# Attention's first q and k loaded raw, with heads on partitions, ahead of a weight fold in a one-core attention and feed-forward kernel

## The chip, the cores and the metric

The kernel runs on one core of a Trainium2 chip. The metric is the device time of one execution in microseconds (us); the median of several executions is quoted. The profile is one such execution; its span (first to last instruction) is about 1.7 us shorter than the time of the same execution (202.8 beside 204.56).

Engines: PE is the matrix engine (TensorE), PEld its weight loads, DVE the vector engine, ACT the scalar engine, POOL the engine that issues the casting loads (the software queue), SP the engine that issues the raw loads, the transposing DMAs and the stores (the hardware queue).

## The reference

```python
# q, k, v: [4 batches, 8 heads, 768 positions, 64], float32
scores = q @ k.T / sqrt(64)                    # keep 4 sink positions and a window of 128
a = softmax(where(keep, scores, -1e9))
x = (a @ v) as [3072 tokens, 512]
out = (((x @ w1) * (x @ w2)) @ w3) @ w_out     # w1, w2 [512,1024], w3 [1024,1024], w_out [1024,512]
```

Nothing nonlinear stands between w3 and w_out, so the kernel first folds them into `w3o = w3 @ w_out` (an extra product at the start, a shorter one for every token afterwards). That fold needs w3 (4 MB) and w_out (2 MB) early. Attention needs only 1.5 MB for its first tile of 256 positions of batch 0 ("tile 0"). These loads share the first 25 us (DMA share 1.13 to 2.13 from 5 to 25 us in the windows of the kernel before; the share is explained there).

## The kernel before

The order of all PE, ACT, DVE and SP instructions is fixed when the program is built: a small model in the kernel guesses when each load lands and how long each step takes, and emits the work in the order of that model. If the matrix engine would idle in the first 40 us by the model, it emits filler matmuls (`keep_busy`, tile `pz`), meant to keep the engine's clock up.

```python
# POOL casts while loading: float32 in memory, bf16 in SBUF
def rows(src, b, kb):                       # 128 positions; runs of 64 floats = 256 B
    return src[b, :, kb * P:(kb + 1) * P, :].rearrange("h p d -> p h d")

order = [('w3', 0, 2, 1, 2), ('w3', 2, 4, 1, 2), ('wo', 1), ('qkv', 0, 0, 2), ('w3', 6, 8, 0, 2),
         ('qkv', 0, 2, 4), ('w3', 5, 6, 0, 2), ('w3', 4, 5, 0, 2), ('w1', 0), ('w2', 0), ('w1', 1),
         ('w2', 1), ('qkv', 0, 4, 6), ('qkv', 1, 0, 6), ('qkv', 2, 0, 6), ('qkv', 3, 0, 6)]
# ... four raw loads on SP, cast afterwards by DVE and ACT:
def load_raw(dst, src, i0, tile_):
    nc.sync.dma_start(out=tile_, in_=src[i0 * P:(i0 + 2) * P, 0:512].rearrange("(ko ki) n -> ki ko n", ki=P))
    return dst[:, i0:i0 + 2, 0:512], tile_
casts = [load_raw(w3_sb, moe_w3, 0, raw(0, 0)), load_raw(wo_sb, moe_w_out, 0, raw(1, 0)),
         load_raw(wo_sb, moe_w_out, 2, raw(1, 1)), load_raw(w3_sb, moe_w3, 2, raw(0, 1))]
# ... cut ...
def transposes(src, dst, t):                # q or k of 256 positions to [head dim, position]
    tp = ps_mm.tile([P, NP, 2, P], BF16, tag="mm", name="tp")
    for r in range(NP):
        for i in range(2):
            nc.tensor.transpose(tp[:, r, i, :], src[:, 2 * t + i, r * P:(r + 1) * P], ident[:])
    yield
    nc.vector.tensor_copy(dst[:, :, t * 256:(t + 1) * 256], tp[:].rearrange("p r i m -> p r (i m)"))
    yield
# ... cut: scores, values, gates, fold, project; the model; the emission ...
```

The softmax here doesn't subtract the row's maximum and nothing guards it: scores larger than these inputs give would overflow.

## Time and profile before

| | before |
|---|---|
| time, median (lowest to highest) | 204.73 us (204.12 to 204.88, 3 runs) |
| span of the profiled execution | 202.2 us |
| last matmul ends | 198.6 us |
| idle + fillers of PE up to 26 us | 4.9 + 9.9 us |
| idle of PE from 26 us to the last matmul | 0.9 us |
| first scores | 24.2 us |

The split into idle, fillers and wanted work is my sum over the trace: a matmul counts from its start to the start of the next one, at most for its own duration; what lies between is idle. (The prediction's own reading of the same timeline, 15.4 and 1.1 us, was done by hand.)

These are lines of the table of windows of the kernel before: the window in us, its length, then busy us and number of instructions of PE, PEld, DVE, ACT, POOL, the granted PE clock as a share of full speed, the DMA share (the times of all packets added up, over 16 engines; packets overlap, and it reaches 2.13 here), and GB/s written. The clock of the first window is not to be trusted: no clock is on record before 5.3 us, and the fillers follow each other every 0.43 us until then and every 0.22 afterwards.

```profile
0.00:5.00 5.00, 3.67 (x9) 1.34 (x10) 2.19 (x5) 1.28 (x1) 3.23 (x9) 1.00 0.56 151
5.00:10.00 5.00, 4.92 (x28) 2.36 (x27) 3.15 (x8) 1.12 (x2) 2.98 (x6) 1.00 1.13 295
10.00:15.00 5.00, 2.36 (x19) 1.32 (x20) 0.77 (x3) 2.01 (x2) 5.00 (x7) 1.00 1.51 223
15.00:20.00 5.00, 5.00 (x33) 2.63 (x33) 1.72 (x8) 0.30 (x1) 4.86 (x8) 1.00 2.13 171
...
25.00:30.00 5.00, 4.95 (x57) 3.30 (x57) 3.79 (x11) 3.15 (x5) 4.53 (x7) 1.00 1.54 194
```

From 25 us on PE is busy all the time; only the start has slack. "Busy" includes fillers, which the timeline of PE separates. It gives start, duration, operation, output and inputs, count, and in brackets the idle time before the group and what ended it:

```profile
1.33 5.98 PE L376 MATMUL pz<-ksbd_113 128*128 128x512 bf16 x18 [1.33 <-DVE ksbd_113 L146]
7.15 0.39 PE L333 MATMUL tp_259<-ident,w_sb 128*128 128x128 bf16 x4
...
13.80 0.40 PE L333 MATMUL tp_291<-ident,w_sb 128*128 128x128 bf16 x4 [1.33 <-ACT w_sb L163]
...
22.17 0.61 PE L191 MATMUL tp<-ident,kN_86 128*128 128x128 bf16 x8
22.62 0.61 PE L191 MATMUL tp<-ident,qN_82 128*128 128x128 bf16 x8
...
24.16 0.51 PE L245 MATMUL sc<-qT_94,kT_98 64*128 64x256 bf16 x8 [0.28 <-DVE qT_94 L194]
```

The fold (`tp_…`, `ph`) comes first and waits piece by piece for weights; q and k of tile 0 are transposed only at 22.2 us. In the first 26 us about 15 us are fillers or idle. That is what a change of the load order can win.

The part of the page that lists DMA issues (size each, median us from issue to landing):

```profile
ab_106<-in_moe_w_dram SPq DMA_DIRECT2D x2, 512.0 KB, 7.5
ab_107<-in_moe_w_out_dram SPq DMA_DIRECT2D x2, 512.0 KB, 6.9
```

Of the four raw 512 KB loads the first landed at 5.4 us and the last at 12.7.

### The profile page before, as it was taken

The numbers are of one execution on the slowest core, as the hardware profiler recorded it, in microseconds if no ns is written. First come the engines' busy times: TensorE is split into PE (matmuls) and PEld (weight loads), VectorE is DVE, ScalarE is ACT, GpSimd is POOL, SyncE is SP. The second block draws the span as 40 slices with busy tenths as digits, with TensorE's granted clock in tenths as the row PEclk, the third lists the DMA queues.
The fourth block names the chain that finished last, engine by engine and source line by source line (L and its number), as shares of the span: only waits on it lengthen the run. The fifth ranks groups of instructions, "written<-read, shape, count | busy, mean of one in ns | idle before, by whom it ended". The sixth has DMA issues, their size and how long they took to land.

```text
span 202.2 us, 4514 instructions
## 1 busy us (share of the span) xinstructions
PE 192.7 (95%) x1800; PEld 120.7 (60%) x1813; DVE 109.9 (54%) x263; ACT 107.0 (53%) x180; POOL 74.1 (37%) x97
## 2 busy tenths in 40 slices
PE   7949899999999999999999999999999999999992
PEld 2425466698886885576666655566665466554440
DVE  4613288665897773467878654877775044440000
ACT  2231556755765866777666664666663433333331
POOL 6699494488999963622770000000000000000000
PEclk9999999999999999999999999999999999999999
DMA  5999999999999999999999994502021610002333
GB/s 154 294 219 173 165 197 206 192 156 154 154 150 151 161 144 126 214 175 204 155 132 157 118 161 129 159 5 52 3 52 67 192 55 2 0 3 104 150 145 120
DMA packets 102773, 27.04 MB, mean 134 GB/s; under 512 B 95072, under 2 KB 98144, under 8 KB 102752
## 3 DMA queue, kind: packets, MB, share of 16 engines
q0 software_dynamic: 78624, 13.64, 91.5%
q1 hardware_dynamic: 24128, 13.11, 29.9%
q8 instruction: 14, 0.23, 0.5%
q14 instruction: 7, 0.06, 0.1%
HBM read 29.36 MB, written 6.29 MB: 176 GB/s over the span
## 4 chain that ended last, share of the span: by engine, by line
PE 87%; DMA 7%; ACT 2%; issue 1%; DVE 1%; SPq 1%; ACTq 0%
PE pg L316 42%; PE po L362 19%; PE av L276 7%; PE sc L245 6%; DMA ab_106<-in_moe_w_dram 5%; PE pw L351 3%; PE tp L191 2%; PE ph L351 2%; DMA xT_104<-xn 2%; PE xt L292 1%; PE pz L376 1%; PE sp L226 1%; ACT w3o L355 1%; SPq L140 1%; ACT w_sb L163 1%
## 5 line engine op out<-in xcount | busy, mean ns | idle before, releaser
L316 PEld LDWEIGHTS <-w_sb 128*128 128x128 bf16 x576 | 53.0, 98 | 25.5 <-issue 1.6
L323 ACT COPY a_sb<-pg 128x384 f32<-128x384 f32 (+1 forms) x72 | 32.0, 445 | 35.2 <-PE pg L316 15.0
L250 ACT ACTIVATE ex<-sc 128x1024 bf16<-128x1024 f32 (+1 forms) x48 | 44.8, 955 | 7.6 <-PE sc L245 7.0
L254 DVE TENSOR_TENSOR am<-ex,maskt 128x1024 bf16<-128x1024 bf16 (+1 forms) x48 | 30.3, 641 | 4.4 <-ACT ex L250 4.2
L366 ACT COPY o_sb<-po 128x512 f32<-128x512 f32 x24 | 14.1, 586 | 26.9 <-PE po L362 26.7
L316 PE MATMUL pg<-xT_102,w_sb 128*128 128x256 bf16 x192 | 24.3, 273 | 0.0
L316 PE MATMUL pg<-xT_103,w_sb 128*128 128x384 bf16 x128 | 23.7, 326 | 0.0
L316 PE MATMUL pg<-xT_104,w_sb 128*128 128x384 bf16 x128 | 22.6, 326 | 0.4 <-DMA xT_104<-xn 0.4
L283 DVE TENSOR_TENSOR xn<-av,rec 128x256 bf16<-128x256 f32 x48 | 20.4, 424 | 4.1 <-DMA xT_104<-xn 2.5
L316 PE MATMUL pg<-xT_105,w_sb 128*128 128x384 bf16 x128 | 21.0, 326 | 0.0
L276 PEld LDWEIGHTS <-am 128*128 128x128 bf16 x352 | 17.0, 97 | 3.3 <-issue 0.3
L320 DVE TENSOR_TENSOR ab_109<-a_sb,pg 128x384 bf16<-128x384 f32 x16 | 8.8, 553 | 17.1 <-PE pg L316 17.1
L280 DVE RECIPROCAL rec<-av 128x4 f32<-128x4 f32 x48 | 8.6, 180 | 16.5 <-PE av L276 16.2
L320 DVE TENSOR_TENSOR ab_106<-a_sb,pg 128x256 bf16<-128x256 f32 x24 | 10.0, 418 | 5.7 <-PE pg L316 4.2
L376 PE MATMUL pz<-ksbd_113 128*128 128x512 bf16 x36 | 10.5, 444 | 1.4 <-DVE ksbd_113 L146 1.3
L362 PE MATMUL po<-w3o,ab_106 128*128 128x512 bf16 x45 | 11.2, 379 | 0.2
L320 DVE TENSOR_TENSOR ab_108<-a_sb,pg 128x384 bf16<-128x384 f32 x16 | 8.9, 554 | 4.4 <-PE pg L316 1.6
L362 PE MATMUL po<-w3o,ab_107 128*128 128x512 bf16 x46 | 10.9, 379 | 0.1
L351 PEld LDWEIGHTS <-w3t 128*128 128x128 bf16 x64 | 6.0, 97 | 8.3 <-issue 2.0
L362 PE MATMUL po<-w3o,ab_108 128*128 128x512 bf16 x46 | 10.6, 379 | 0.1
L362 PE MATMUL po<-w3o,ab_109 128*128 128x512 bf16 x47 | 10.5, 379 | 0.1
L320 DVE TENSOR_TENSOR ab_107<-a_sb,pg 128x384 bf16<-128x384 f32 x16 | 8.8, 552 | 2.7 <-ACT ex L250 1.5
(143 smaller groups left out, 254.4 us busy)
## 6 DMA issues: line engine op xcount, KB each, us to landing
out_dram<-o_sb SPq DMA_DIRECT2D x24, 256.0 KB, 2.1
w_sb<-in_moe_w_dram POOLq DMA_DIRECT2D x5, 512.0 KB, 10.1
ab_106<-in_moe_w_dram SPq DMA_DIRECT2D x2, 512.0 KB, 7.5
w_sb<-in_moe_w_dram POOLq DMA_DIRECT2D x4, 256.0 KB, 8.3
ab_107<-in_moe_w_out_dram SPq DMA_DIRECT2D x2, 512.0 KB, 6.9
kN_86<-in_k_dram POOLq DMA_DIRECT2D x6, 128.0 KB, 8.8
qN_82<-in_q_dram POOLq DMA_DIRECT2D x6, 128.0 KB, 8.6
vN_90<-in_v_dram POOLq DMA_DIRECT2D x6, 128.0 KB, 8.5
```

Source lines behind the costliest of these rows:

```text
L245: nc.tensor.matmul(sc[:, e, c:c + n], kT[b][hp, r, kb * P:(kb + 1) * P], qT[b][hp, r, qb * P:qb * P + n], start=True, stop=True)
L250: nc.scalar.activation(ex[:, :, c0:], sc[:, :, c0:], ACTF.Exp, scale=scale)
L254: nc.vector.tensor_mul(am[:, :, c0:], ex[:, :, c0:], mk)
L276: nc.tensor.matmul(o, lhs, rhs, start=(n == 0), stop=(n == len(todo) - 1), skip_group_check=True)
L283: nc.vector.tensor_mul(xns[b, t][:, :, r, :, :], av[:, :, :, 0:D], rec[:].to_broadcast([P, 2, 2, D]))
L316: nc.tensor.matmul(pg[:], w_sb[:, kk, dt * P:(dt + 1) * P], xT[b][:, kk, tk], start=(kk == 0), stop=(kk == NP - 1))
L320: nc.vector.tensor_mul(ab[b][:, dt, tk], gate_a.pop((b, c, dt))[:], pg[:])
L323: nc.scalar.copy(a_sb[:], pg[:])
L351: nc.tensor.matmul(po, w3T[i][:, j, :], wo_sb[:, j, :], start=(j == 0), stop=(j == KFF - 1))
L362: nc.tensor.matmul(po[:], ab[b][:, kk, m * P:(m + 1) * P], w3o[:, kk, :], start=(kk == 0), stop=(kk == KFF - 1))
L366: nc.scalar.copy(o_sb[:], po[:])
L376: nc.tensor.matmul(pz[:], idle[:, 0:P], idle[:, 0:512], start=True, stop=True)
```

## The change

The intent: start with attention instead of the fold. k and q of tile 0 are loaded raw (float32, no cast) as the first two loads, in runs of 16 rows (4 KB). Partition p then holds head p // 16 and the run p % 16 of that head. PE transposes these tiles in float32, and the copies out of PSUM ("untangle") put the columns in order and cast them. Both DVE and ACT copy from each PSUM tile. w3 comes by whole rows of blocks, w_out in two column halves so that half a fold can start, w1 and w2 in quarters, and the other q, k of batch 0 in 512 B runs of two positions ("paired").

```diff
+    def run(src, b, t):
+        return src[b, :, 256 * t:256 * t + 256, :].rearrange("h (g j) d -> h g (j d)", j=16)
+
+    def pairs(src, b, t):
+        return src[b, :, 256 * t:256 * t + 256, :].rearrange("h (p j) d -> p h (j d)", j=2)
 ...
-    order = [('w3', 0, 2, 1, 2), ('w3', 2, 4, 1, 2), ('wo', 1), ('qkv', 0, 0, 2), ...
+    raw_order = [("k",), ("q",), ("w3", 0)]
+    order = [("w3", 2), ("wo", 0, 256), ("w3", 6), ("w3", 5), ("v", 0, 0), ("w3", 3), ("wo", 256, 512), ("w2", 0,
+             256), ("w1", 0, 256), ("w3", 1), ("k", 0, 1), ("q", 0, 1), ("w1", 256, 512), ("w3", 7), ...
 ...
+            nc.sync.dma_start(out=raw(n), in_=run({"k": k, "q": q}[what], 0, 0))
 ...
+    def transposes_raw(src, part, box):          # two parts of four, for k and for q
+        tp = ps_mm.tile([P, 4, P], FP32, tag="mm", name="tpr")
+        for n in range(4):
+            c = (4 * part + n) * P
+            nc.tensor.transpose(tp[:, n, :], src[:, c:c + P], ident32[:])
+        box.append(tp)
+        yield
+
+    def untangle(dst, part, e, box):             # e = 0 on DVE, e = 1 on ACT, same tile
+        tv = box[0][:].rearrange("p n (r e g) -> p e r g n", r=NP, e=2)
+        dv = dst[:, :, 0:256].rearrange("p r (g n j) -> p r g n j", g=16, n=8)
+        for j in range(2):
+            (nc.scalar.copy if e else nc.vector.tensor_copy)(
+                dv[64 * e:64 * e + 64, :, :, 4 * part:4 * part + 4, j], tv[64 * j:64 * j + 64, e])
+        yield
 ...  (cut: paired transposes, fold in column halves with the copy on DVE or ACT, sink scores
       merged into the scores task, new landing model and priorities)
```

## The prediction

> **What bounds the kernel now.** The table of windows has TensorE busy about 98% from 26 to 198.6 us: that part is its own work. The start is not: the timeline of TensorE up to 26 us holds about 10.6 us of wanted matmuls (weight transposes 8 x 0.22, fold matmuls 4 x 1.73, sink values 0.23, q/k transposes 0.9, scores 0.44). The other 15.4 us are idle or fillers (group pz; 18 of them fill 1.3 to 7.1 us). Later idle time is about 1.1 us, then 3.5 us of tail. Span 202.2 = 15.4 + about 182 useful + 1.1 + 3.5. Only the 15.4 us can be attacked.
>
> The start waits for data: the raw weight loads land at 5.4, 7.0, 9.9 and 12.7 us, the first q and k only at about 22. The windows show about 155 GB/s written while q, k, v come in 256-byte destination rows, 205 for casting weight rows; a casting load reads twice what it writes, so 0.31 and 0.41 MB/us are read, about 0.33 in the mixed raw stage.
>
> **What changes.** Raw k and q of tile 0 come first, so attention can start before the fold; w3 comes by rows, w_out in two column halves, so that half a fold (0.86 us) can run on half of w_out; w1, w2 in quarters; other batch-0 q, k in 512-byte source runs; the weight casts (3 x 1.04 us on ACT) go.
>
> Added TensorE work: 24 fp32 transposes, estimated at twice a bf16 one (0.055 us pipelined), +1.3 us; paired transposes, 16 instead of 8 per tile and tensor, four times, +0 to +1.8 us. Sink scores and values cost the same. About +2 us, all on the critical engine.
>
> **Start, worked out from those rates.** k lands at 5.2 to 6.5 us, q at 7 to 9: [...] these loads may get 8 engines of 16. No run yet shows it. First w_out half about 13 us, v of tile 0 about 17.5, second half about 22. By then about 11 us of work can be done; after that the backlog of second halves (4 to 5 us), the first gates and later w3 rows should keep TensorE full. So 11 to 12 us not useful instead of 15.4: 3.5 to 4.5 saved, about 2 given back; a little more from fewer small gaps and retuned priorities. Later stages unchanged within 1 us, whatever ACT and DVE save, because TensorE is full.
>
> **Prediction: 201.6 us, 198.6 to 204.4 (8 in 10). Faster by over 2%: 0.33; within 2%: 0.64; slower by over 2%: 0.03.**
>
> **What would show it.** First wanted matmul near 6 us instead of 7.1; first scores at 9 to 11 us instead of 24; first av at 17 to 19; fillers plus idle up to 26 us about 12; TensorE full from about 22 us; an fp32 transpose near 0.11 us pipelined; later stages as before.
>
> **What would make it wrong.** Faster: larger runs give 0.4 MB/us from the start, so w_out and v come 2 to 3 us earlier; paired transposes overlap fully. Slower: [...] raw loads crowd the casting queue; the strided untangling copies hold PSUM; landing guesses miss and TensorE stalls in its static order.

3.5 to 4.5 us saved less about 2 given back is 1.5 to 2.5 us, and the "little more" makes up the rest of the way from 204.7 to 201.6. The landings and the factor of two for a float32 transpose were my estimates; the factor was borne out by the runs (0.109 us each in g16_part, 0.056 for a bf16 one in the kernel before).

## The result

| | before | after |
|---|---|---|
| time, median (lowest to highest) | 204.43 us (203.76 to 204.88, 4 runs) | 210.11 us (209.61 to 211.29, 4 runs) |
| ratio of the fast runs | | 1.0294, interval 1.0256 to 1.0332 |
| span of the profiled execution | 202.2 us | 208.7 us |
| first scores | 24.2 us | one matmul at 19.2 us, the others from 20.2 |
| PE idle + fillers up to 26 us | 4.9 + 9.9 us | 8.7 + 8.5 us |

A ratio is the mean time of one kernel's fast runs over that of the other's of the same rounds, so it is not quite the ratio of the medians. The change made the kernel 2.9% slower. The prediction (201.6, range 198.6 to 204.4) was wrong.

The same windows after:

```profile
0.00:5.00 5.00, 3.67 (x10) 1.38 (x11) 2.92 (x11) 1.28 (x1) 3.81 (x11) 1.00 0.43 94
5.00:10.00 5.00, 2.78 (x17) 1.61 (x16) 0.08 (x1) 0.41 (x1) 4.95 (x10) 1.00 1.20 209
10.00:15.00 5.00, 1.29 (x6) 0.39 (x4) 2.01 (x8) 1.30 (x4) 0.76 (x1) 0.97 1.58 189
15.00:20.00 5.00, 3.98 (x25) 3.63 (x26) 2.51 (x6) 1.57 (x4) 0.81 (x2) 0.69 1.43 206
...
25.00:30.00 5.00, 4.54 (x65) 3.69 (x63) 3.48 (x11) 2.55 (x4) 1.82 (x3) 1.00 1.44 198
```

PE is less busy than before from 5 to 20 us, and the granted clock falls (0.69 in 15 to 20 us). The timeline of PE says what it waited for:

```profile
1.33 5.38 PE L428 MATMUL pz<-ksbd 128*128 128x512 bf16 x17 [1.33 <-DVE ksbd L170]
8.93 1.06 PE L246 MATMUL tpr<-ident,ab 128*128 128x128 f32 x8 [2.22 <-DMA ab<-in_k_dram]
9.83 1.46 PE L428 MATMUL pz<-ksbd 128*128 128x512 bf16 x6
15.38 1.94 PE L246 MATMUL tpr<-ident,ab 128*128 128x128 f32 x8 [4.09 <-DMA ab<-in_q_dram]
17.11 1.98 PE L393 MATMUL tp<-ident,ab 128*128 128x128 bf16 x16
19.23 0.27 PE L300 MATMUL sc<-qT,kT 64*128 64x256 bf16 x1
20.18 0.49 PE L300 MATMUL sc<-qT,kT 64*128 64x256 bf16 x7 [0.68 <-ACT qT L255]
...
22.65 1.92 PE L404 MATMUL pw<-wo_sb,w3t 128*128 128x256 bf16 x16
```

k landed at 8.9 us and q at 15.3, where 5.2 to 6.5 and 7 to 9 were predicted. The same eight transposes took 1.06 us for k and 1.94 for q, because the clock had halved meanwhile (0.5 on record from 14.7 to 18.1 us). The fold products (`pw`) start only at 22.7 us. That is not w_out's doing alone: its first half landed at 18.4 us, and from then on PE works, in its fixed order, through w3's transposes, the scores with their wait for q's copies, and 1.7 us of fillers. The chain of waits of the changed kernel has the same three parts in order (start, duration, what):

```profile
1.66 13.58 DMA ab<-in_q_dram
15.24 0.14 issue
15.38 1.10 PE tpr L246 x4
16.48 0.02 issue
16.50 0.42 ACT qT L255
...
17.40 0.42 DVE qT L255
...
19.27 0.42 ACT qT L255
```

So there are three suspects: the load of q (13.6 us from issue to landing), the copies, in which ACT and DVE take turns (16.50 to 20.14 us for q), and the clock. Wanted PE work also grew. Sums over all matmuls of the profiled executions, as defined above:

| us | before | after | g16 | g16_part |
|---|---|---|---|---|
| idle, before the last matmul | 4.6 + first 1.3 | 8.1 + 1.3 | 3.6 + 1.3 | 1.6 + 1.3 |
| fillers | 9.9 | 8.5 | 10.9 | 8.8 |
| wanted work | 182.9 | 187.2 | 187.4 | 185.9 |
| of it: transposes of q and k on PE | 5.6 | 7.6 | 6.7 | 6.7 |
| of it: transposes of w3 | 3.9 | 4.7 | 5.0 | 4.4 |
| last matmul ends | 198.6 | 205.1 | 203.3 | 197.6 |

(12 of the 256 fold and project matmuls of the kernel before are missing from its trace, which hides some tenths of a us of its work. The runs g16 and g16_part are explained below; the profiled execution of g16 is the slowest of its five, 208.67 us, and that of g16_part the fastest of its four, so these two columns lie further apart than the medians.)

### The profile page after: what moved, and what is told of

It is laid out like the page before. It is cut to its first block, busy times and chain, and to the rows that moved or that the text cites. A ratio compares the mean times of both kernels' runs of the same rounds, so it can differ in the third digit from the quotient of the medians.

```text
span 208.7 us, 4640 instructions
## 1 busy us (share of the span) xinstructions
PE 195.7 (94%) x1862; PEld 127.3 (61%) x1862; DVE 115.5 (55%) x273; ACT 106.7 (51%) x183; POOL 71.2 (34%) x96
## 4 chain that ended last, share of the span: by engine, by line
PE 85%; DMA 7%; DVE 5%; ACT 1%; issue 0%; SPq 0%; ACTq 0%; DVEq 0%
PE pg L374 40%; PE po L414 20%; PE pw L404 7%; PE av L334 7%; DMA ab<-in_q_dram 7%; PE sc L300 6%; PE xt L350 1%; PE tp L220 1%; DVE qT L255 1%; ACT qT L255 1%; PE tp L234 1%; PE pz L428 1%; PE tp L393 1%; PE sp L294 1%; DVE kT L237 1%; PE tpr L246 1%
## 5 line engine op out<-in xcount | busy, mean ns | idle before, releaser
L374 PE MATMUL pg<-xT,w_sb 128*128 128x384 bf16 (+1 forms) x576 | 90.1, 308 | 0.1
L378 DVE TENSOR_TENSOR ab<-a_sb,pg 128x384 bf16<-128x384 f32 (+1 forms) x72 | 36.4, 508 | 28.2 <-PE pg L374 26.5
L414 PE MATMUL po<-w3o,ab 128*128 128x512 bf16 x192 | 43.7, 379 | 0.3 <-DVE qT L223 0.3
L414 PEld LDWEIGHTS <-ab 128*128 128x128 bf16 x192 | 18.2, 98 | 20.4 <-issue 0.4
L341 DVE TENSOR_TENSOR xn<-av,rec 128x256 bf16<-128x256 f32 x48 | 20.4, 425 | 1.7
L114 POOL DMA_DIRECT2D qN<-in_q_dram x18 | 16.3, 905 | 9.5 <-DMA vN<-in_v_dram 4.4
L334 PE MATMUL av<-vN,am 128*128 128x65 bf16 x352 | 19.1, 193 | 0.1
L114 POOL DMA_DIRECT2D vN<-in_v_dram x18 | 16.1, 918 | 7.4 <-DMA kN<-in_k_dram 7.2
L338 DVE RECIPROCAL rec<-av 128x4 f32<-128x4 f32 x48 | 8.6, 178 | 18.1 <-PE av L334 18.0
L114 POOL DMA_DIRECT2D kN<-in_k_dram x18 | 16.3, 910 | 4.0 <-DMA qN<-in_q_dram 2.9
L404 PE MATMUL pw<-wo_sb,w3t 128*128 128x256 bf16 x128 | 15.4, 273 | 0.2 <-DVE w3t L213 0.2
L300 PE MATMUL sc<-qT,kT 64*128 64x128 bf16 (+1 forms) x256 | 14.3, 238 | 0.9 <-ACT qT L255 0.7
L404 PEld LDWEIGHTS <-w3t 128*128 128x128 bf16 x128 | 11.9, 98 | 2.4 <-DVE w3t L213 0.5
## 6 DMA issues: line engine op xcount, KB each, us to landing
w_sb<-in_moe_w_dram POOLq DMA_DIRECT2D x8, 256.0 KB, 10.4
```

The source lines that it names most:

```text
L114: nc.gpsimd.dma_start(out=dst, in_=rows(src, b, kb))
L300: nc.tensor.matmul(sc[:, e, c:c + n], kT[b][hp, r, kb * P:(kb + 1) * P], qT[b][hp, r, qb * P:qb * P + n], start=True, stop=True)
L334: nc.tensor.matmul(o, lhs, rhs, start=(n == 0), stop=(n == len(todo) - 1), skip_group_check=True)
L341: nc.vector.tensor_mul(xns[b, t][:, :, r, :, :], av[:, :, :, 0:D], rec[:].to_broadcast([P, 2, 2, D]))
L374: nc.tensor.matmul(pg[:], w_sb[:, kk, dt * P:(dt + 1) * P], xT[b][:, kk, tk], start=(kk == 0), stop=(kk == NP - 1))
L378: nc.vector.tensor_mul(ab[b][:, dt, tk], gate_a.pop((b, c, dt))[:], pg[:])
```

## Experiments

Theory, a guess of mine before the runs: how many DMA engines a load gets goes with its slowest dimension. The two loads have 8 heads there, so k and q would run on 8 of the 16 engines, and everything queued behind them on those 8 would be late too. Rivals: the casting queue crowds the raw loads; the landing guesses make PE stall in a bad order; the raw form (float32 transposes, copies) or attention first is itself the loss; the layout (a head's runs on neighbouring partitions) is slow.

### g16: the 16 runs of a head slowest

```diff
-  rearrange("h (g j) d -> h g (j d)", j=16)     # source [8, 16, 1024]
+  rearrange("h (g j) d -> g h (j d)", j=16)     # source [16, 8, 1024]
-  tv = box[0][:].rearrange("p n (r e g) -> p e r g n", r=NP, e=2)
+  tv = box[0][:].rearrange("p n (g r e) -> p e r g n", r=NP, e=2)
```

> The changed kernel with one thing altered: raw k and q of tile 0 lie on the partitions with the 16 runs of a head as the slow dimension and the 8 heads as the fast one (slowest dimension of the source 16 instead of 8), untangled accordingly. Same bytes, same runs, same instructions. Theory (the two loads run on 8 of the 16 DMA engines, and everything queued behind them on those 8 is late too): k lands at 5.2 to 6 us instead of 8.9, q at 7 to 8 instead of 15.3, the first w_out half at about 13 to 14 instead of 18.6, the clock does not fall, and the time is 200 to 203.5 us. Rival (the casting queue crowds the raw loads, or the extra fp32 work costs the time): q still lands after 12 us and the time is 208 us or more.

Measured: 207.43 us (206.99 to 208.67), ratio 1.0118 (1.0080 to 1.0156). Lines of its issues (size, us to landing), k issued at 0.80 and q at 1.55 us:

```profile
ab<-in_k_dram SPq DMA_DIRECT2D x1, 512.0 KB, 4.8
ab<-in_q_dram SPq DMA_DIRECT2D x1, 512.0 KB, 7.3
```

k lands at 5.6 us and q at 8.9: the landing part of the theory holds, and crowding alone is refuted, since the casting queue was the same. The order of the 1862 matmuls of PE is the same in both traces, so no change of order hides in the difference. But the time fell by 2.7 us only, and the clock fell in spite of the expectation (0.5 from 14 to 20.8 us in the profiled execution, the slowest; by their mean clock of 0.988 to 0.992 the other four lost less). Something else held PE. Its trace shows the copies in turns, and PE waiting for them:

```profile
12.63 0.86 ACT L255 CAST qT<-tpr 64x256 bf16<-64x256 f32 x2
...
13.53 1.77 DVE L255 CAST qT<-tpr 64x256 bf16<-64x256 f32 x4 [1.87 <-ACT qT L255]
14.54 1.08 PE L393 MATMUL tp<-ident,ab 128*128 128x128 f32 x4 [1.22 <-DVE qT L255]
15.39 0.86 ACT L255 CAST qT<-tpr 64x256 bf16<-64x256 f32 x2 [1.89 <-DVE qT L255]
```

Fillers that the program placed for the full clock then ran at the half one and stood in the way: seven took 3.17 us here, and 1.69 in the changed kernel.

```profile
17.03 3.17 PE L428 MATMUL pz<-ksbd 128*128 128x512 bf16 x7
```

### g16_part: g16, and one engine for each PSUM tile

```diff
-  (nc.scalar.copy if e else nc.vector.tensor_copy)(...)      # each tile by both engines
+  for e in range(2):
+      (nc.scalar.copy if part else nc.vector.tensor_copy)(...)  # part 0: DVE, part 1: ACT
```

> As g16, and each PSUM tile of raw transposes is untangled by one engine alone (part 0 by the vector engine, part 1 by the scalar engine, four copies each) instead of by both. In the changed kernel the two engines took turns, 0.86 us each, never at once, although planned as parallel. If they take turns because they read one PSUM tile, they now overlap, q is ready about 1.7 us earlier, and the time falls by 0 to 1 us against g16. If they take turns because both write interleaved places of one destination tile, they still take turns, and the time is that of g16 within 0.5 us.

Measured: 203.92 us (202.94 to 204.82), ratio 0.9955 (0.9903 to 1.0007): 3.5 us below g16, more than the 0 to 1 expected. The copies now overlap (10.80 to 12.57 and 10.95 to 12.69 us) although both engines write interleaved places of one tile, so the shared PSUM tile was the cause of the turns:

```profile
10.80 1.77 DVE L254 CAST qT<-tpr 64x256 bf16<-64x256 f32 x4
10.95 1.74 ACT L254 CAST qT<-tpr 64x256 bf16<-64x256 f32 x4 [0.41 <-PE tpr L246]
```

The turns are in the program: the trace of the changed kernel has semaphore waits between the two engines at this line, which g16_part has not. Ready q moves from 16.25 to 12.69 us. But the 3.5 us are not the copies' alone: the profiled execution of g16 loses the clock too, and the edit also changed the durations in the program's model, so that from about the 60th matmul on the order of PE differs (two fillers fewer, and the first fold product ahead of the second scores). The shares were not separated. The expectation had missed that k's copies and q's queue behind each other, and that the clock would fall where PE waits for them (in g16 to 0.5 from 14 us on, amid waits of 1.14 and 1.22 us).

```profile
12.74 0.66 PE L392 MATMUL tp<-ident,ab 128*128 128x128 f32 x4 [0.93 <-ACT qT L254]
13.33 0.50 PE L299 MATMUL sc<-qT,kT 64*128 64x256 bf16 x8
...
14.86 1.04 PE L403 MATMUL pw<-wo_sb,w3t 128*128 128x256 bf16 x8
```

### part8: the copies alone

The changed kernel with the edit of g16_part but the 8 heads still slowest (PE's order is that of g16_part, matmul by matmul).

> The changed kernel with only the untangling split by part (one engine for each PSUM tile); the loads keep 8 heads as slowest dimension. k and q land as in the changed kernel (8.9 and 15.3 us); the eight copies of q take about 1.8 us after the transposes instead of 3.6. If the turns on one PSUM tile cost time of their own, 1 to 2.5 us are saved against the changed kernel (time 207.5 to 209); if only the landing of q matters, the time stays within 0.7 us of it.

Measured: 209.92 us (209.62 to 210.76), ratio 1.0284 (1.0251 to 1.0318), 0.2 us below the changed kernel. q's copies end at 18.44 instead of 20.13 us, but the clock was at one half from 13.5 to 20.3 us and PE was still transposing w3 until 19.6. So with q late the edit gains nothing clear of noise; part of the reason is that clock, at which w3's transposes took 3.16 us instead of 1.98. Beside g16_part, which has the same order of PE, the slowest dimension alone is worth 6.0 us. The two faults are not additive: mending one gives 2.7 us, the other 0.2, both 6.2 (differences of medians from 210.11).

### hold and hold2: nothing beside the raw loads

In `hold` a copy on POOL that reads raw q stands ahead of the casting loads. In `hold2` the casting loads are also pinned behind that copy.

```diff
+    hold = nc.gpsimd.tensor_copy(held[:], raw_t0["q"][:, 0:H])
+    behind = tc.issue_after(hold.ins)     # hold2 only; entered here, left after the last load
```

> The changed kernel (8 heads slowest) with the casting queue held until raw q has landed, so that nothing but the raw loads is in the DMA engines until then. Theory of half the engines: at most 8 packets of k and q in flight, k lands at 6.3 to 7.3 us, q at 9 to 10, so still 1.5 to 3 us later than 16 engines would; the casting loads then come later and the time is 206 to 212 us. Rival (crowding by the casting queue alone): k lands at 5.2 to 5.6, q at 6.5 to 7.2 us, as the raw loads of the kernel before.

Measured: 214.47 us (214.06 to 214.87), ratio 1.0471 (1.0435 to 1.0506). The build had moved the first two casting loads (1.5 MB read) ahead of the copy, so it did not test what it said: k landed at 8.8 and q at 14.0 us, later than either side expected of an empty queue. The time is above the expected range too, since nothing but two casting loads was started in the first 14 us.

> As the run called hold, but with all the casting loads really behind the wait for raw q (in hold two of them, 1.5 MB read, had been moved ahead of it, so hold tested less than it said). k and q now share the DMA engines only with raw w3 row 0. Theory of half the engines: at most about 8 packets of k and q at once, k lands at 6 to 7.5 us, q at 8.5 to 11. Rival (crowding by the casting queue): k at 5.2 to 5.7, q at 6.5 to 7.2. Time over 213 us, of no interest.

Measured (one look): 209.47 us, not the over 213 expected; k was there by 7.8 us (PE did not wait for it), q at 10.9. With 8 slowest and no casting load beside it, q is thus there at 10.9 (the second raw load of the kernel before, as large and with 128 as slowest dimension, landed at 7.0); with the casting loads beside it, it is there 4.4 us later, at 15.3. With 16 slowest (g16), the same casting loads and nothing held, q is there at 8.9. In hold2 the casting loads start ten us later (11.0 instead of 1.3 us), yet this one time is no worse than that of the changed kernel.

The trace has a record for each packet of 4 KB. The 384 raw packets of k, q and w3, in order of their start, can be counted in groups of 64: how many are in flight at once. While w3's packets are among them, that is 17 to 19 in each of these runs; what tells the runs apart is the stretch after that.

| run | slowest dimension of k, q | packets | us | most at once | mean at once | median ns of a packet |
|---|---|---|---|---|---|---|
| after | 8 | 193 to 256 | 7.3 to 10.6 | 9 | 5.6 | 281 |
| after | 8 | 321 to 384 | 13.2 to 16.2 | 8 | 5.3 | 176 |
| hold2 | 8 | 257 to 320 | 7.8 to 9.3 | 10 | 7.2 | 160 |
| g16 | 16 | 193 to 256 | 6.4 to 7.8 | 18 | 12.3 | 276 |
| g16 | 16 | 321 to 384 | 8.7 to 9.9 | 16 | 9.5 | 172 |

The trace also has, for each load, the updates of its semaphore that came from DMA. Their number goes with that of the packets at once: 8 updates where the last packets are at most 8 to 10 at once, 16 where they are 16 to 18 (not so in perhead, below: 16 updates for each small load of k, but 3 to 5 packets at once on average). I take it for the number of engines that a load runs on. That is my reading, since the trace does not name the engine of a packet; "8 engines" and "16 engines" stand for these two figures.

| run | updates for k (us) | for q | for raw w3 |
|---|---|---|---|
| after | 8 (7.2 to 8.8) | 8 (13.6 to 15.2) | 8 (8.3 to 8.9) and 8 (15.6 to 16.6) |
| hold2 | 8 (5.9 to 7.7) | 8 (9.2 to 10.8) | 8 (7.5 to 8.0) and 8 (10.4 to 11.8) |
| g16 | 16 (5.3 to 5.6) | 16 (8.3 to 8.8) | 16 (9.9 to 10.3) |
| g16_halves (below; two loads each) | 8 (5.3 to 6.2) and 8 (9.4 to 10.1) | 8 (12.2 to 12.8) and 8 (15.6 to 15.9) | 8 (11.9 to 12.9) and 8 (17.1 to 17.4) |

(Each load with 8 has one more update, 1.0 to 1.3 us after its issue. For k of the changed kernel it comes at 2.0 us, before the first packet starts at 2.3, so it tells of no data.) In the changed kernel half of w3's updates come long before q's and half after them, as they would if half of its engines were free of k and q; which engines they were is not shown.

### told: measured landings in the model

```diff
+    arrive["raw", "k"], arrive["raw", "q"], arrive["raw", "w3", 0] = 8.9, 15.3, 16.7
```

> The changed kernel whose order of work is laid out with the measured landings of the raw loads (k 8.9, q 15.3, w3 16.7 us) instead of guessed ones; the transfers are untouched. If the wrong guesses made the engines stall in a bad order, the time falls to 204 to 206.5 us. If the data are simply late, it stays at 207.5 us or more, at most 2.5 us gained by fillers that keep the clock up.

Measured: 212.02 us (211.30 to 212.90), ratio 1.0353 (1.0311 to 1.0396): slower still. This order, with three of the landings put right, does not help; it put fold products early that then waited 3.1 us for w_out (until 18.6 us), whose landing was still guessed, and q's transposes only at 21.5 us. An order made for all the measured landings was not tried, so how much of the loss it could save stays open.

### warm: fillers in the gap

Eighteen more fillers ahead of q's raw transposes.

> The changed kernel with 18 more fillers on the matrix engine ahead of the raw transposes of q, which cover the 4.1 us in which it idled there. The granted clock, which fell to one half from about 14.6 to 18.3 us, should stay at 1.0; transposes of q and w3 row 0 then take 1.0 us for eight instead of 1.9. If the lower clock lengthens the critical chain, 0.5 to 1.5 us are saved (time 208.5 to 209.7); if it hid behind the untangling copies, under 0.5.

Measured: 209.99 us (209.69 to 210.64), ratio 1.0285 (1.0253 to 1.0318). The clock stayed up and q's transposes took 1.06 us again, but the time is that of the changed kernel. In the profiled executions q's copies start at 15.99 instead of 16.50 us and the fold at 22.14 instead of 22.65, so the lower clock cost 0.5 us there and the rest hid behind the copies; the medians do not show even that.

```profile
9.54 5.34 PE L428 MATMUL pz<-ksbd 128*128 128x512 bf16 x24
15.32 1.06 PE L246 MATMUL tpr<-ident,ab 128*128 128x128 f32 x8 [0.44 <-DMA ab<-in_q_dram]
```

### noraw and noraw2: q and k of tile 0 through the casting queue

```diff
-    raw_order = [("k",), ("q",), ("w3", 0)]
+    raw_order = [("w3", 0)]
-    order = [("w3", 2), ...
+    order = [("k", 0, 0), ("q", 0, 0), ("w3", 2), ...
-        kN[0][:, 0:2, :].rearrange("p i n -> p (i n)")]            # noraw2 only: place of w3 row block 7
+        ab[0][:].rearrange("p k s -> p (k s)")[:, 2048:2048 + DF]]
```

> The changed kernel with one part of the change undone: k and q of tile 0 come through the casting queue in 512-byte runs with the pairing of rows, first in that queue, and only w3 row 0 comes raw. No load has 8 as slowest dimension at 16 engines' cost in 4 KB runs, no fp32 transposes of q and k, no shared PSUM tile. Theory (raw form and its 8 engines are the loss, the order attention first is sound): k and q land at 6 to 9 us, first scores at 10 to 12, and the time is 200.5 to 204.5, at or below the kernel before. Rival (attention first is itself the loss): over 206 us.

Measured: 226.61 us. The run is void, by my mistake: w3 row block 7 (the expectation of noraw2 calls it row 1) is loaded into the place that the changed kernel no longer needs for k, and here it is needed. PE waited 22.2 us for that load, and by the order of the program the transposes then read w3 in place of k. (It still passed the comparison with the reference, so that comparison is a weak test of q and k; presumably the scores of these inputs are too small to matter, which was not checked. I checked the reordering in g16 by hand, index by index.)

> The run noraw was void: w3 row 1 was loaded into the place where k of tile 0 now lies, so k's transposes waited for it (22 us) and read the wrong data. Here w3 row 1 goes to a free place. k and q of tile 0 come first in the casting queue, 512-byte runs, paired. They land at 6 to 9 us; the casting loads behind them at most 2 us later than in g16_part. Theory (the raw form and its 8 engines are the loss, attention first is sound): 200.5 to 204.5 us. Rival (attention first is the loss): over 206.

Measured: 203.86 us (203.39 to 204.27), ratio 0.9989 (0.9952 to 1.0026), within the range expected. k and q were transposed at 8.5 and 9.6 us and the scores started at 11.9. So attention first is no loss, and does not need the raw form; it is no gain either.

### perhead: eight small loads

Raw k and q as eight loads of one head each, layout unchanged.

> The changed kernel with raw k and q each as eight loads of one head (16 partitions, 16 runs of 4 KB) in place of one load of eight heads; same layout, same untangling. A second way to the 16 engines that leaves the layout as it was. Theory: up to 16 or more packets at once; the issues take about 0.45 us each, so k is issued by 4.4 and q by 8 us; q lands at 9.5 to 11.5 instead of 15.3, the first w_out half well before 18.6, and the time is near that of g16 (207.4): 206 to 209. Rival (the layout with a head's runs on neighbouring partitions is what is slow, not the number of engines): q still after 14 us and 210 us or more.

Measured: 212.38 us (211.69 to 212.69), ratio 1.0396 (1.0353 to 1.0439), outside the range of the theory. The eight issues for q took from 4.5 to 11.9 us, q landed at 17.9, and packets were only 3 to 5 at once on average. Issuing was not the limit at first: k's eight loads, each with 16 updates, were issued by 4.1 us, and the last of them landed only at 11.5. What held them is not shown (each writes 16 neighbouring partitions), so this run does not tell layout from engines apart.

### g16_halves: the layout of g16, slowest dimension 8 again

```diff
-  nc.sync.dma_start(out=raw(n), in_=run(..., 0, 0))
+  for g in (0, 8):
+      nc.sync.dma_start(out=raw(n)[8 * g:8 * g + 64], in_=run(..., 0, 0)[g:g + 8])
```

> g16 (layout with the 8 heads fast and the 16 runs of a head slow), but each raw load of k and q cut into two loads of 8 runs by 8 heads, so that the slowest dimension is 8 again. Layout, packets and untangling as in g16; two more issues of about 0.5 us. If the number of engines is the cause: after raw w3 is through its share at most about 8 to 10 packets at once, q lands at 13 us or later, time 209 us or more. If the layout was the cause: q lands at 9 to 10.5 us and the time is within 1.5 us of g16 (207.4).

Measured: 211.97 us (211.70 to 212.19), ratio 1.0379 (1.0337 to 1.0420). q lands at 15.9 us:

```profile
10.27 1.07 PE L247 MATMUL tpr<-ident,ab 128*128 128x128 f32 x8 [3.50 <-DMA ab<-in_k_dram]
11.17 2.50 PE L429 MATMUL pz<-ksbd 128*128 128x512 bf16 x6
16.02 1.94 PE L247 MATMUL tpr<-ident,ab 128*128 128x128 f32 x8 [2.36 <-DMA ab<-in_q_dram]
```

Same layout, same packets, same bytes as g16; only the slowest dimension went from 16 to 8 (with one more issue per tensor), and q went from 8.9 to 15.9 us. The last raw packets are again at most 8 to 10 at once. So the slowest dimension alone is enough to make q late, and the layout is not needed to explain it. Whether the old layout would be slow on 16 engines too is not excluded (perhead).

### unpaired, fewfill, best: what is left to win

> g16_part with the other q, k of batch 0 loaded in 256-byte runs again and transposed in 8 instead of 16 pieces. Saves about 0.12 us of matrix-engine time four times[...]. Time that of g16_part (203.9) less 0.5, give or take 1.

Measured: 203.01 us (202.70 to 203.25), ratio 0.9947 (0.9914 to 0.9981).

> g16_part with 11 instead of 17 fillers before the raw transposes of k. There the fillers ran at 0.43 us each while the clock was low and ended at 7.9 us, though k had landed at 5.9. If this delay reaches the end, 0.5 to 1.5 us are saved (202.4 to 203.4); if the later wait for q and w_out absorbs it, nothing; if the shorter warm-up leaves the clock low, it is slower than g16_part.

Measured: 203.37 us (202.43 to 204.24), ratio 0.9965 (0.9917 to 1.0013); against g16_part not told apart from scatter.

> g16_part with both unpaired and fewfill. If their gains add, 202.2 to 203.0 us, ratio to the kernel before 0.989 to 0.994; if both were scatter, 203 to 204.

Measured: 203.42 us (202.84 to 204.26) in 5 fast runs, with one slow run of 205.97 left out; ratio 0.9964 (0.9921 to 1.0008). The gains do not add; by the expectation this is the outcome of two gains that were scatter. unpaired is the fastest version found, about 0.5% under the kernel before and clear of it by its own interval, but best, which contains it, is not; it is far from the 2% that one would like to see.

## Why the prediction was wrong

- **What bounds the kernel: right.** Only the start can be attacked. Idle time of PE after 26 us is 0.9 us before and 0.7 after.
- **Added PE work: right in size, about +2 us.** g16_part, whose clock stayed up, has 3.1 us more wanted work than the kernel before, of which 1.2 us lie in the fold and project products, partly because 12 of them are missing from the latter's trace. Transposes of q and k cost 1.1 us more (6.7 against 5.6) and those of w3 0.5 more; an eight-fold float32 transposition takes 0.87 us of pipelined time (0.109 each, twice the 0.056 of a bf16 one), as predicted; a paired tile 0.57 instead of 0.45. The changed kernel has 1.3 us more than g16_part (187.2 against 185.9), nearly all of it in transposes that ran at the lower clock.
- **The step that failed: "k lands at 5.2 to 6.5 us, q at 7 to 9 ... First w_out half about 13 us".** I had guessed at the 8 engines, but estimated their effect as up to 1 or 2 us, for these two loads alone. Measured: k 8.9, q 15.3. With 8 slowest and the casting queue held, q comes at 10.9 (hold2), with that queue running at 15.3 (after). Loads of the casting queue came late too, and this the prediction left out: the first w_out half, v of tile 0 and the second half landed at 18.4, 22.6 and 26.5 us, where 13, 17.5 and 22 were predicted. With 16 slowest (g16) they landed at 12.4, 16.6 and 20.4, and k and q at 5.6 and 8.8: the predicted times were nearly those of that run. (That the late loads wait for their share on the engines of k and q is my reading; g16 shows only that they come earlier when k and q do.) So 17.2 us up to 26 us were not useful instead of 11 to 12. g16 and g16_halves, which have the same order of PE, show the cause, the slowest dimension, in both directions (q at 8.9 and at 15.9 us).
- **A term not in the sum: the copies.** I listed the strided copies as a risk because of PSUM, and the kernel's own model plans DVE and ACT in parallel, 0.36 to 0.4 us a copy. They took 0.43 us each, and the program made the two engines take turns on one PSUM tile, 3.6 us for q instead of 1.8. With q on time the edit that mends this gains 3.5 us (g16 against g16_part), the clock and a changed order of PE included.
- **A term not in the sum: the clock.** PE idles from 11.3 to 15.4 us and its clock is at one half from 14.7 to 18.1. By itself that cost nothing that the medians show in the changed kernel, and 0.5 us in its profile (warm).
- **What the sum was worth with both faults mended.** g16_part has 11.4 us of idle time and fillers up to 26 us, where I had predicted 11 to 12, w_out in use at 14.9 us and sink values of v at 18.0. Yet it runs in 203.9 us, not 201.6. Its fastest execution took 202.94 and had the span of 201.2 that these sums describe; the others were up to 1.9 us longer, and the profiles of those were not kept. What made them longer stays open. The warm-up varies (in the profiled runs the clock reached full speed anywhere between 4.0 and 7.2 us, and the 17 first fillers took 5.4 us in one run and 6.7 in another), but it hardly explains it: the fastest execution was a late one, 6.8 us. A later drop of the clock does not either, since the mean clock of the others was 0.997 to 1.0.

What stays open besides: which of the engines a load ran on is not in the trace; shown are the numbers of updates (8 or 16) and of packets at once (8 to 10 or 16 to 18), and the effect of the slowest dimension (q at 15.3 or 8.9 us). Why 4 KB packets took about 280 to 360 ns in the crowded stages and 160 to 176 in the empty ones was not tried.

## What to carry to other kernels

Look at the slowest dimension of a DMA's source before anything else: here the same bytes in the same 4 KB runs landed at 8.9 us with 16 there and at 15.3 with 8, and with 8 the first w_out half, in the other queue, landed at 18.4 instead of 12.4. When two engines are to empty PSUM together, give each its own tile and check in the trace that their copies overlap (here q's copies took 1.8 us so, and 3.6 from shared tiles). A reordering that starts earlier but adds work to the bounding engine has to win back that work first: here 3 to 4 us of idle time won and 2 to 3 us of work added left at most about half a per cent.
